# Pooled attention and two gated MLPs on one core: the second MLP's weight loads in pieces of 32 rows, low parts of the spatial inputs by VectorE, and another order of all steps

## The chip, the cores and the metric

The kernel runs on one core of a Trainium2 chip. The metric is the device time of one execution in microseconds (us). A core has five engines with their own instruction queues: TensorE (PE in the profile, with its weight loads as PEld), VectorE (DVE), ScalarE (ACT), GpSimd (POOL) and SyncE (SP), which here only starts DMA transfers. TensorE's clock has two levels, 1.2 and 2.4 GHz; the profile shows which share of full speed was granted (PEclk).

## The reference

Batch 8, sequence 576, width 512, 1024 inner columns. Three parts follow each other:

```python
# 1: attention over keys and values pooled by 8 (8 heads of 64)
attn = softmax(scale * q @ mean8(k).T);  x = attn @ mean8(v)
# 2: MLP with a gate from a convolution over the sequence
h = relu(x @ w_in)
g = h * sigmoid(conv3(h, conv_w));       x = g @ w_out
# 3: MLP with a spatial gate
h = gelu_tanh(x @ w_in2);  u, v = halves of h
v_n = (v - mean) / sqrt(var + 1e-6) * g_ln
v_s = einsum('ts,bsd->btd', w_sg, v_n) + b_sg
out = x + (u * v_s) @ w_out2
```

The weights come as 64-bit floats; the kernel reads them as pairs of 32-bit words and makes fp32 values of them with three integer instructions of VectorE (`to_f32`: one per line 146, 149 and 152).

## The kernel before, in words

Products run in fp32r, a format with fewer bits than fp32. To keep the precision each operand x is split into a high part h (a ScalarE cast) and a low part l = x - h (a subtraction, helper `subtract`, line 134, so every such subtraction stands at L134 in the profile), and a product takes three matmuls, hh, lh and hl. The tables `LO_X`, `LO_S`, `LO_G` and others (lines 109 to 114) name the engine that makes the low part of each operand: VectorE (`dve`) or GpSimd (`pool`).

Part 1 works batch by batch (steps k, v, q, s, e, a), and part 2 in 12 chunks of 384 columns. `t_i(f, c)` is the product of filter block f with chunk c, 12 matmuls into a bank of PSUM tag "i" (two banks, psi), and its epilogue: ScalarE's relu and centre tap, VectorE's two other taps (L569, L570), ScalarE's tanh, VectorE's g (L576, the last reader of the bank), then hg's high part on ScalarE and its low part on GpSimd. `t_o(f, c)` adds g @ w_out with 9 matmuls (L99 to L101) and writes the chunk to DRAM (`x2s`, L605).

When the attention is done, its SBUF tiles are released and the pool "w2" takes their place (`t_att_close`). Then `t_w2` loads the second MLP's input weight in eight pieces (w2raw, 512 KB each: half e of the columns, the rows of block kt) and converts each with three instructions of VectorE. Each half has three raw buffers for four loads, so the fourth load waits until the first is converted. `t_wsum` (GpSimd) and `t_wsplit` (ScalarE, VectorE) then make the seven combined weights of a Strassen-like scheme in which a 2 x 2 block product takes seven products (`products`). All this stands between chunks 9 to 11 of part 2.

Part 3 then reads x2s back transposed (`t_x2`), makes the seven combined inputs (`t_xc`), and computes u and v (`t_u`, `t_v2`), both stored to DRAM. The spatial stage goes by batch: `t_sc` makes seven combined spatial inputs sc of the normalised v, each a high and a low part; `t_sp` multiplies them with w_sg; its results gate u on GpSimd (L979); `t_g` splits the gated u into high and low parts (g for four full blocks of 128 rows, gr for the rest of 64 rows), and `t_o2` is the last product with the residual.

What sets the order: the string `ORDER` holds 3,617 steps. Each step is one call to `step`, which runs one generator up to its next `yield`, and every instruction that it issues is tied to the one before it on the same engine:

```python
            if ins.engine in last:
                tc.add_manual_dep(ins, last[ins.engine], pin, reason="order")
```

So each engine, and SyncE's queue of DMA issues, works strictly in the written order; a waiting instruction holds all that stand behind it on its engine. Semaphores between the engines follow from the data and from the buffers.

Of the kernel before, what the change touches and what calls it, by code (L numbers as in the profile page):

```python
# [26 lines left out]
def pooled_attention_gated_mlps(  # L27
# [23 lines left out]
    nc = tc.nc  # L51
    w_in, conv_w, w_out, w_in2, w_out2 = (a.bitcast(U32) for a in (w_in, conv_w, w_out, w_in2, w_out2))
    B, H, S, D = q.shape
# [6 lines left out]
    KC = DM // 128  # L60
# [5 lines left out]
    NM = S // 128  # L66
# [22 lines left out]
    def a_bank():  # L89
        return psum1.tile([128, 512], F32, tag="a", bufs=3, name="psa")  # L90
# [7 lines left out]
    def mm3(out_, ah, al, bh, bl, first, last):  # L98
        nc.tensor.matmul(out=out_, lhsT=ah, rhs=bh, start=first, stop=False)  # L99
        nc.tensor.matmul(out=out_, lhsT=al, rhs=bh, start=False, stop=False)  # L100
        nc.tensor.matmul(out=out_, lhsT=ah, rhs=bl, start=False, stop=last)  # L101

    def mm_sum(out_, pairs):
        n = len(pairs)
        for i, (a, b_) in enumerate(pairs):
            nc.tensor.matmul(out=out_, lhsT=a, rhs=b_, start=(i == 0), stop=(i == n - 1))  # L106

    dve, pool = nc.vector, nc.gpsimd
    LO_IN = [pool for f in range(NF)]
    LO_OUT = [pool for f in range(NF)]  # L110
    LO_E = [pool for b in range(B)]
    LO_X = {1: dve, 2: dve, 3: dve, 4: dve, 5: dve, 6: pool, 7: pool}
    LO_S = {1: dve, 2: dve, 3: pool, 4: dve, 5: dve, 6: dve, 7: pool}
    LO_G = [dve, dve, dve, pool, pool]
    ident = const.tile([128, 128], F32, name="ident")
    small = const.tile([128, 6], F32, name="small")
    mask, mhalf = small[0:96, 0:4], small[:, 4:6]
    coef = const.tile([128, 32], F32, name="coef")

    in1_ctx = ExitStack()  # L120
    in1 = in1_ctx.enter_context(tc.tile_pool(name="in1", bufs=1))
    att_ctx = ExitStack()
    att1 = att_ctx.enter_context(tc.tile_pool(name="att1", bufs=1, side="right"))
    att2 = att_ctx.enter_context(tc.tile_pool(name="att2", bufs=2, side="right"))
    KBT = att1.tile([128, NP_, 2 * SP], F32, name="KBT")
# [7 lines left out]
    def subtract(out, in0, hi, eng=nc.vector):  # L133
        eng.tensor_tensor(out=out, in0=in0, in1=hi.bitcast(F32), op=ALU.subtract)  # L134

    def to_f32(raw, t, tmp=None):

        w = raw.rearrange("p (n t) -> p t n", t=2)
        lo, up = w[:, 0, :], w[:, 1, :]
        ti = t.bitcast(U32)
        mi = ti if tmp is None else tmp.bitcast(U32)
        nc.vector.tensor_scalar(out=mi, in0=up, scalar1=3, scalar2=0x3FFFFFF8,
                                op0=ALU.logical_shift_left, op1=ALU.bitwise_and)
        yield
        nc.vector.scalar_tensor_tensor(out=mi, in0=up, scalar=0xC0000000, in1=mi,
                                       op0=ALU.bitwise_and, op1=ALU.bitwise_or)  # L150
        yield
        nc.vector.scalar_tensor_tensor(out=ti, in0=lo, scalar=29, in1=mi,
                                       op0=ALU.logical_shift_right, op1=ALU.bitwise_or)
        yield
# [454 lines left out]
    w2 = {}  # L609
# [5 lines left out]
    def split(dst, x, eng):  # L615
        nc.scalar.copy(out=dst[:, 0], in_=x)  # L616
        yield
        subtract(dst[:, 1], x, dst[:, 0], eng)
# [8 lines left out]
    def t_w2(i, *_):  # L627
        kt, e = i % KC, i // KC
        p = w2["p"]
        raw = p.tile([128, 1024], U32, tag=f"c{e}{4 + kt % 3}", name="w2raw")  # L630
        nc.sync.dma_start(
            out=raw, in_=w_in2[:, 1024 * e:1024 * e + 1024].rearrange("(c k i) n -> k c i n", k=KC, i=32)[kt])
        yield
        if kt % 2 == 0:
            wf[e, kt // 2] = p.tile([128, 2, 512], F32, tag=f"c{e}{kt // 2}", name="w2f")
        yield from to_f32(raw, wf[e, kt // 2][:, kt % 2, :], a_bank())
# [279 lines left out]
    def t_sc(m, b):  # L916
# [11 lines left out]
        sc[b, m] = w2["p"].tile([128, 2, 2, FH], F32R, tag=f"c0{m - 1}", name="sc")  # L928
        yield from split(sc[b, m], x, LO_S[m])

# [7 lines left out]
    g2 = {}  # L938
# [44 lines left out]
    def t_g(i, b):  # L983
# [12 lines left out]
        for h, l, y in hl:  # L996
            subtract(l, y, h, LO_G[i])

# [21 lines left out]
    def t_o2(i, b):  # L1020
# [14 lines left out]
        else:  # L1035
            for e in range(2):
# [4 lines left out]
    tasks = {"z": t_setup, "c": t_coef, "i": t_w_in, "t": t_w_out, "k": t_k, "K": t_kfin, "v": t_v, "V": t_vfin,  # L1041
             "q": t_q, "p": t_qtr, "s": t_s, "e": t_e, "x": t_x, "h": t_hg, "a": t_a, "I": t_i, "O": t_o, "A": t_att_close,
             "w": t_w2, "W": t_wsum, "Q": t_wsplit, "B": t_x2_open, "y": t_x2, "T": t_xc, "n": t_v2, "u": t_u,
             "g": t_sg, "G": t_sgsum, "H": t_sgsplit, "J": t_sgrest, "l": t_w_out2, "L": t_load, "S": t_sc, "R": t_vr,
             "b": t_bsg, "U": t_uload, "d": t_sp, "D": t_g, "m": t_res, "o": t_o2}
# [5 lines left out]
    def step(key):  # L1051

        if key not in running:
            i, _, b = key[1:].partition(".")
            running[key] = iter(tasks[key[0]](int(i or 0), int(b or 0)) or ())
        more = next(running[key], 0)
        issued = nc.cur_bb.bb.instructions
        for n in range(seen[0], len(issued)):
            ins = issued[n]
            if ins.engine in last:  # L1060
                tc.add_manual_dep(ins, last[ins.engine], pin, reason="order")
            last[ins.engine] = ins.name
        seen[0] = len(issued)
        return more is None

    for key in ORDER.split():
        step(key)
# [30 lines left out]
```

## Time and profile before

| | |
|---|---|
| median of 3 runs | 1012.65 us (1009.92 to 1012.85) |
| the profiled execution's own time | 1012.78 us |
| its span, first to last instruction | 1010.6 us |
| mean granted TensorE clock | 0.974 |
| busy TensorE / VectorE / GpSimd / ScalarE | 935.9 / 788.5 / 610.3 / 530.2 us |

The profile is of one execution. Names are out<-in with buffer numbers left out (w2raw is the weight piece of `t_w2`; in_moe_w_in_dram stands for both MLPs' input weights, since digits are dropped). A DMA share of 1 would be all 16 DMA engines busy. Where a busy TensorE runs at a granted clock below 1.00, its busy time is longer for the same work, so matmul counts are to be read beside it.

### The profile page before, as it was taken

The page shows a single profiled execution, that of the slowest core. Times are in us where ns is not written, and L with a number is a line of the kernel's source. Part 1 is how long each engine was busy: PE and PEld are TensorE (multiplying, and loading weights), DVE is VectorE, ACT ScalarE, POOL GpSimd, SP SyncE. Part 2 cuts the span into 40 slices and gives each one's busy share as a digit, 9 for nine tenths or more (in the row PEclk, how much of TensorE's full clock was granted, in tenths as well). Part 3 has the DMA queues.
Part 4 walks back from the last instruction along what each step waited for, and adds up shares of the span by engine and source line. Part 5 has one row for each costly group of instructions (what it writes and reads, how often), then busy time and mean ns, then how long its engine had stood idle before and what let it go on. Part 6 is the DMA issues. An engine that isn't in the chain of part 4 may idle for free.

```text
span 1010.6 us, 15826 instructions
## 1 busy us (share of the span) xinstructions
PE 935.9 (93%) x5396; PEld 853.9 (85%) x5396; DVE 788.5 (78%) x1351; ACT 530.2 (52%) x1108; POOL 610.3 (60%) x678
## 2 busy tenths in 40 slices
PE   5888899999999999999769979899899879999998
PEld 5786789899898998988658879889899869999996
DVE  5979987979888788886458469899776997767763
ACT  3755667676767667666236447556555332322211
POOL 3788687777777675473134256354542887776652
PEclk9899999999999999999779989999999999999999
DMA  9964263755637373231210574675366646565644
GB/s 241 269 195 95 79 151 102 169 149 132 171 108 163 87 153 108 66 103 59 104 59 32 100 118 119 160 199 129 112 171 220 205 138 184 179 206 172 202 141 135
DMA packets 182220, 143.60 MB, mean 142 GB/s; under 512 B 99296, under 2 KB 136444, under 8 KB 182140
## 3 DMA queue, kind: packets, MB, share of 16 engines
q1 hardware_dynamic: 182140, 142.61, 52.2%
q8 instruction: 42, 0.69, 0.3%
q14 instruction: 38, 0.31, 0.1%
HBM read 94.20 MB, written 48.37 MB: 141 GB/s over the span
## 4 chain that ended last, share of the span: by engine, by line
PE 62%; DVE 12%; POOL 7%; DMA 7%; SPq 4%; issue 3%; ACT 3%; POOLq 0%; DVEq 0%; ACTq 0%
PE psi L106 15%; PE pso L745 9%; PE psa L745 8%; PE pso L99 5%; PE pso L101 5%; PE pso L100 5%; DMA w2raw<-in_moe_w_in_dram 4%; PE psi L100 3%; PE psi L99 3%; PE psi L101 3%; PE psa L106 3%; PE psa L418 3%; POOL xb L692 1%; DVE vg L790 1%; DMA st<-in_v_dram 1%
## 5 line engine op out<-in xcount | busy, mean ns | idle before, releaser
L134 POOL TENSOR_TENSOR hg<-g,hg 128x384 fp32r<-128x384 f32 x96 | 101.7, 1064 | 91.2 <-ACT hg L579 91.0
L569 DVE SCALAR_TENSOR_TENSOR psi<-h,coef,psi 128x384 f32<-128x384 f32 x96 | 58.8, 612 | 36.7 <-ACT psi L567 35.9
L979 POOL TENSOR_TENSOR u<-u,tmp 128x288 f32<-128x288 f32 x64 | 61.6, 978 | 35.2 <-DVE tmp L975 24.8
L692 POOL TENSOR_TENSOR xb<-xb 128x768 f32<-128x768 f32 x24 | 47.8, 1996 | 56.5 <-DMA wsg<-in_moe_w_sg_dram 20.2
L572 ACT ACTIVATE psi<-psi 128x384 f32<-128x384 f32 x96 | 46.5, 484 | 63.4 <-DVE psi L570 63.2
L557 ACT ACTIVATE h<-psi 128x386 f32<-128x386 f32 (+1 forms) x96 | 47.3, 493 | 49.8 <-PE psi L106 49.6
L134 POOL TENSOR_TENSOR eTl<-xb,eTh 128x512 fp32r<-128x512 f32 (+1 forms) x30 | 44.9, 1496 | 44.1 <-ACT eTh L502 37.7
L570 DVE SCALAR_TENSOR_TENSOR psi<-h,coef,psi 128x384 f32<-128x384 f32 x96 | 59.8, 623 | 3.4
L576 DVE SCALAR_TENSOR_TENSOR g<-psi,h 128x384 f32<-128x384 f32 x96 | 52.4, 546 | 10.2 <-ACT psi L572 8.6
L579 ACT CAST hg<-g 128x384 fp32r<-128x384 f32 x96 | 47.9, 506 | 21.1 <-DVE g L576 20.7
L418 PE MATMUL psa<-KBT,qT 128*128 128x144 f32 (+1 forms) x320 | 54.8, 303 | 4.4 <-DVE eTl L134 2.1
L616 ACT CAST sc<-vf 128x512 fp32r<-128x512 f32 x48 | 29.0, 619 | 56.7 <-POOL vf L926 30.3
L745 PE MATMUL psa<-wc,xc 128*128 128x256 f32 x378 | 51.8, 284 | 7.0 <-DVE vg L773 6.7
L567 ACT ACTIVATE psi<-h,coef 128x384 f32<-128x384 f32 x96 | 56.3, 586 | 3.1
L745 PE MATMUL pso<-wc,xc 128*128 128x256 f32 x378 | 54.3, 293 | 3.3 <-ACT tmp L768 2.3
L745 PE MATMUL psa<-xc,wc 128*128 128x384 f32 x252 | 51.6, 348 | 5.4 <-ACT tmp L812 2.2
L418 PEld LDWEIGHTS psa<-KBT,qT 128*128 128x128 f32 (+1 forms) x320 | 46.3, 188 | 11.8 <-issue 2.9
L745 PEld LDWEIGHTS psa<-wc,xc 128*128 128x128 f32 x378 | 49.2, 189 | 8.1 <-DVE vg L773 7.3
L745 PEld LDWEIGHTS pso<-wc,xc 128*128 128x128 f32 x378 | 51.8, 198 | 4.2 <-ACT tmp L768 2.5
L745 PE MATMUL pso<-xc,wc 128*128 128x384 f32 x252 | 49.2, 338 | 2.8 <-DVE ub L822 2.2
L745 PEld LDWEIGHTS psa<-xc,wc 128*128 128x128 f32 x252 | 44.9, 197 | 6.9 <-ACT tmp L812 2.6
L697 ACT CAST xc<-xb 128x768 fp32r<-128x768 f32 x42 | 34.4, 836 | 27.8 <-POOL xb L692 13.8
(398 smaller groups left out, 3182.4 us busy)
## 6 DMA issues: line engine op xcount, KB each, us to landing
xb<-eds SPq DMA_DIRECT2D x24, 384.0 KB
x2s<-ob SPq DMA_DIRECT2D x36, 256.0 KB
xb<-x2s SPq DMA_DIRECT2D x48, 192.0 KB
us<-ub SPq DMA_DIRECT2D x24, 384.0 KB
vs<-vg SPq DMA_DIRECT2D x18, 512.0 KB
u<-us SPq DMA_DIRECT2D x16, 576.0 KB
vf<-vs SPq DMA_DIRECT2D x16, 512.0 KB
out_dram<-ob SPq DMA_DIRECT2D x32, 256.0 KB
```

Of the source, the lines that this page charges most:

```text
L99: nc.tensor.matmul(out=out_, lhsT=ah, rhs=bh, start=first, stop=False)
L100: nc.tensor.matmul(out=out_, lhsT=al, rhs=bh, start=False, stop=False)
L101: nc.tensor.matmul(out=out_, lhsT=ah, rhs=bl, start=False, stop=last)
L106: nc.tensor.matmul(out=out_, lhsT=a, rhs=b_, start=(i == 0), stop=(i == n - 1))
L134: eng.tensor_tensor(out=out, in0=in0, in1=hi.bitcast(F32), op=ALU.subtract)
L418: nc.tensor.matmul(out=ps[0:n, 2 * SP * x:2 * SP * x + 2 * SP], lhsT=qT[:, p, 0:n], rhs=KBT[:, p, :], start=True, stop=True)
L567: nc.scalar.activation(out=y, in_=tap(1), func=AF.Copy, scale=cw(1, f))
L569: nc.vector.scalar_tensor_tensor(out=y, in0=tap(0), scalar=cw(0, f), in1=y, op0=ALU.mult, op1=ALU.add)
L570: nc.vector.scalar_tensor_tensor(out=y, in0=tap(2), scalar=cw(2, f), in1=y, op0=ALU.mult, op1=ALU.add)
L692: pool.tensor_tensor(out=x, in0=y, in1=z, op=ALU.subtract)
L745: nc.tensor.matmul(out=ps, lhsT=a, rhs=b_, start=first and i == 0, stop=last and i == n - 1, skip_group_check=True)
L979: pool.tensor_tensor(out=z, in0=z, in1=o, op=ALU.mult)
```

## The change

`t_w2` issues four DMAs per load, each of 32 rows into 32 partitions, instead of one whose source is a pattern of 4 blocks by 32 rows. The low parts of all spatial inputs sc and of all gated blocks g and gr are made by VectorE; before, GpSimd made sc of products 3 and 7, the fourth g and gr. And `ORDER` is another sequence of the same 3,617 steps.

```diff
-ORDER = '''z k0.0 k1.0 k2.0 z z p0.0 c p1.0 p2.0 v0.0 v1.0 p3.0 p4.0 v2.0 i0 i1 z z k0.1 k1.0 k2.0
...
+ORDER = '''z k0.0 k1.0 k2.0 z z p0.0 c p1.0 p2.0 v0.0 v1.0 p3.0 p4.0 v2.0 i0 i1 z z k0.1 k1.0 p0.1
...
-    LO_S = {1: dve, 2: dve, 3: pool, 4: dve, 5: dve, 6: dve, 7: pool}
-    LO_G = [dve, dve, dve, pool, pool]
+    LO_S = {m: dve for m in range(1, 8)}
+    LO_G = [dve for i in range(NM + 1)]
...
-        nc.sync.dma_start(
-            out=raw, in_=w_in2[:, 1024 * e:1024 * e + 1024].rearrange("(c k i) n -> k c i n", k=KC, i=32)[kt])
+        for c in range(4):
+            r0 = 128 * c + 32 * kt
+            nc.sync.dma_start(out=raw[32 * c:32 * c + 32], in_=w_in2[r0:r0 + 32, 1024 * e:1024 * e + 1024])
```

SyncE's queue at the end of the attention, before (-) and after (+), eds and xb being attention's scores on their way through DRAM and x2s the chunks of part 2:

```order
+L605 DMA x2s_82<-ob 128x512
 L466 DMA eds_118<-en 64x4x128
 L467 DMA eds_118<-en 64x4x64
 L496 DMA xb<-eds_118 128x384
 L605 DMA x2s_83<-ob 128x512 x2
-L631 DMA w2raw<-in_moe_w_in_dram 128x1x1024 x8
+L633 DMA w2raw<-in_moe_w_in_dram 32x1024 x32
 L605 DMA x2s_83<-ob 128x512
 L605 DMA x2s_84<-ob 128x512 x3
 L605 DMA x2s_85<-ob 128x512 x3
```

The eight loads become 32 issues at the same place; the third store of the same chunk stands behind them in both.

VectorE at the first two conversions of w2raw, before (numbers tell buffers apart: w2raw_5385 is the first load, w2raw_5404 the second, w2raw_5416 the third; psi and g belong to the epilogues of part 2):

```order
L576 SCALAR_TENSOR_TENSOR g_5419<-psi_5388,h_5401 128x384
L146 TENSOR_SCALAR psa_5425<-w2raw_5385 128x512
L149 SCALAR_TENSOR_TENSOR psa_5425<-w2raw_5385,psa_5425 128x512
L146 TENSOR_SCALAR psa_5457<-w2raw_5404 128x512
L152 SCALAR_TENSOR_TENSOR w2f_5424<-w2raw_5385,psa_5425 128x512
L569 SCALAR_TENSOR_TENSOR psi_5440<-h_5453,coef_121,psi_5440 128x384
L570 SCALAR_TENSOR_TENSOR psi_5440<-h_5453,coef_121,psi_5440 128x384
L149 SCALAR_TENSOR_TENSOR psa_5457<-w2raw_5404,psa_5457 128x512
L146 TENSOR_SCALAR psa_5464<-w2raw_5416 128x512
L152 SCALAR_TENSOR_TENSOR w2f_5456<-w2raw_5404,psa_5457 128x512
L576 SCALAR_TENSOR_TENSOR g_5482<-psi_5440,h_5453 128x384
```

The same place after (w2raw_5424 is the first load, w2raw_5433 the second; xl is the low part of an attention output):

```order
L576 SCALAR_TENSOR_TENSOR g_5422<-psi_5335,h_5367 128x384
L146 TENSOR_SCALAR psa_5430<-w2raw_5424 128x512
L149 SCALAR_TENSOR_TENSOR psa_5430<-w2raw_5424,psa_5430 128x512
L152 SCALAR_TENSOR_TENSOR w2f_5429<-w2raw_5424,psa_5430 128x512
L532 SCALAR_TENSOR_TENSOR xl_489<-psa_5358,xh_372 128x288
L146 TENSOR_SCALAR psa_5458<-w2raw_5433 128x512
L576 SCALAR_TENSOR_TENSOR g_5471<-psi_5389,h_5402 128x384
L569 SCALAR_TENSOR_TENSOR psi_5440<-h_5453,coef_121,psi_5440 128x384
L570 SCALAR_TENSOR_TENSOR psi_5440<-h_5453,coef_121,psi_5440 128x384
L149 SCALAR_TENSOR_TENSOR psa_5458<-w2raw_5433,psa_5458 128x512
L576 SCALAR_TENSOR_TENSOR g_5497<-psi_5440,h_5453 128x384
L152 SCALAR_TENSOR_TENSOR w2f_5457<-w2raw_5433,psa_5458 128x512
```

Before, the first instruction of the second load stands ahead of the next epilogue, and that of the third ahead of that epilogue's g; after, the first load is converted in one go, and a whole epilogue stands between the first and the last instruction of the second load.

GpSimd at the end of the first combined inputs of batch 1 and the first gated blocks of batch 0, before (vf and sf are spatial inputs, u the gated product):

```order
L926 TENSOR_TENSOR vf<-sf,vf 128x2x256
L979 TENSOR_TENSOR u_8283<-u_8283,tmp_8591 128x288
L979 TENSOR_TENSOR u_8315<-u_8315,tmp_8568 128x288
L926 TENSOR_TENSOR vf<-vf 128x2x256
L134 TENSOR_TENSOR sc<-vf,sc 128x512 x2
L134 TENSOR_TENSOR g<-u_8315,g 128x2x128
L134 TENSOR_TENSOR g<-u_8283,g 128x2x128
L134 TENSOR_TENSOR gr<-u_8315,gr 128x2x64
L134 TENSOR_TENSOR gr<-u_8283,gr 128x2x64
L979 TENSOR_TENSOR u_8542<-u_8542,tmp_8728 128x288
```

The same place after:

```order
L927 TENSOR_TENSOR vf<-sf,vf 128x2x256
L980 TENSOR_TENSOR u_8475<-u_8475,tmp_8546 128x288
L980 TENSOR_TENSOR u_8305<-u_8305,tmp_8611 128x288
L980 TENSOR_TENSOR u_8475<-u_8475,tmp_8572 128x288
L927 TENSOR_TENSOR vf<-vf 128x2x256
L927 TENSOR_TENSOR sf<-vf 128x512
L980 TENSOR_TENSOR u_8751<-u_8751,tmp_8717 128x288
```

The four kinds of L134 rows are gone from GpSimd; they stand among VectorE's instructions now, and the sums for the next batch follow at once.

## Rows read from the trace of the kernel before

**Rows 1.** the page, head and section 1

```profile
span 1010.6 us, 15826 instructions
PE 935.9 (93%) x5396; PEld 853.9 (85%) x5396; DVE 788.5 (78%) x1351; ACT 530.2 (52%) x1108; POOL 610.3 (60%) x678
```

**Rows 2.** stretches: us; PE, PEld, DVE, ACT, POOL busy (count); PEclk, DMA share, GB/s

```profile
25.00:150.00 125.00, 108.32 (x648) 93.74 (x647) 111.71 (x207) 76.33 (x175) 96.74 (x126) 0.93 0.63 156
150.00:475.00 325.00, 324.65 (x1756) 294.63 (x1755) 267.08 (x493) 221.21 (x441) 223.95 (x276) 1.00 0.47 122
475.00:530.00 55.00, 38.45 (x160) 34.35 (x159) 29.31 (x51) 18.28 (x38) 11.87 (x12) 0.81 0.21 81
530.00:565.00 35.00, 34.71 (x173) 31.05 (x172) 26.67 (x38) 22.21 (x45) 16.31 (x13) 1.00 0.06 23
785.00:835.00 50.00, 41.77 (x275) 39.01 (x276) 48.84 (x78) 17.62 (x39) 40.61 (x37) 0.97 0.56 173
835.00:1000.00 165.00, 165.00 (x970) 149.51 (x969) 113.91 (x189) 45.62 (x111) 108.32 (x110) 1.00 0.59 182
```

**Rows 3.** chain of waits, 470 to 600 us; start us, us, what

```profile
475.42 17.47 DMA w2raw<-in_moe_w_in_dram
495.39 22.92 DMA w2raw<-in_moe_w_in_dram
```

**Rows 4.** waits, 470 to 530 us; us in total, times, longest us

```profile
DVE psa L146 <- DMA w2raw<-in_moe_w_in_dram: 22.1, 6, 6.7
PE psi L106 <- DVE g L576: 16.5, 4, 6.9
```

**Rows 5.** timeline of VectorE; start us, us, what, [idle before <- releaser]

```profile
482.81 0.70 DVE L146 TENSOR_SCALAR psa<-w2raw 128x512 uint32<-128x512 uint32 x1 [2.88 <-DMA w2raw<-in_moe_w_in_dram]
498.00 0.69 DVE L146 TENSOR_SCALAR psa<-w2raw 128x512 uint32<-128x512 uint32 x1 [0.97 <-DMA w2raw<-in_moe_w_in_dram]
```

**Rows 6.** timeline of SyncE's queue, 465 to 540 us

```profile
474.13 25.66 SPq L631 DMA_DIRECT2D w2raw<-in_moe_w_in_dram  x8
499.83 37.51 SPq L605 DMA_DIRECT2D x2s<-ob  x4
```

**Rows 7.** busy time by stretch; and SyncE's v loads, ns min/median/max

```profile
495.00:500.00 5.00, 5.00 (x16) 5.00 (x17) 3.86 (x7) 1.65 (x4) 1.01 (x1) 0.50 0.25 102
676.00:678.00 2.00, 2.00 (x19) 1.99 (x18) 2.00 (x5) 1.16 (x4) 0.00 (x0) 1.00 1.04 405
233.00:238.00 5.00, 5.00 (x25) 4.34 (x24) 4.86 (x11) 3.42 (x7) 2.92 (x4) 1.00 0.64 198
L233 SPq DMA_DIRECT2D raw<-in_v_dram x48: 311/425/1801, 66.2 to 355.7; - x48
```

**Rows 8.** line L134, whole span; duration ns min/median/max, first and last start us

```profile
L134 DVE TENSOR_TENSOR g<-u,g x48: 409/694/1516, 819.4 to 996.0; 128x256 fp32r<-128x256 f32 x48
L134 DVE TENSOR_TENSOR sc<-vf,sc x32: 657/808/1774, 772.8 to 979.8; 128x512 fp32r<-128x512 f32 x32
L134 POOL TENSOR_TENSOR sc<-vf,sc x16: 1280/1402/1804, 790.7 to 967.0; 128x512 fp32r<-128x512 f32 x16
L134 POOL TENSOR_TENSOR g<-u,g x16: 732/742/1189, 819.1 to 993.6; 128x256 fp32r<-128x256 f32 x16
L134 POOL TENSOR_TENSOR gr<-u,gr x16: 454/462/907, 820.9 to 994.7; 128x128 fp32r<-128x128 f32 x16
```

**Rows 9.** by line and shape, 785 to 835 us; busy us, mean ns, idle before

```profile
L134 DVE TENSOR_TENSOR sc<-vf,sc 128x512 fp32r<-128x512 f32 x8 | 10.1, 1262 | 0.0
L134 DVE TENSOR_TENSOR g<-u,g 128x256 fp32r<-128x256 f32 x7 | 6.8, 1005 | 0.0
L134 POOL TENSOR_TENSOR sc<-vf,sc 128x512 fp32r<-128x512 f32 x4 | 6.2, 1574 | 0.0
```

**Rows 10.** chain of waits, 792 to 832 us

```profile
812.27 1.70 POOL sc L134
```

**Rows 11.** busy time by stretch, 715 to 720 us

```profile
715.00:720.00 5.00, 2.28 (x15) 1.87 (x13) 4.57 (x4) 1.63 (x3) 4.74 (x4) 1.00 0.00 0
```

2 lines of the change are left out of this document (1 added, 1 removed).

## The prediction, made before the changed kernel was run

> **What bounds the kernel now.** I read the page's first two sections, then the busy time of each engine by stretch, then the chain of waits and the list of waits in the one long stretch where TensorE is not full, and last the two stretches at 785 us and after it. TensorE is busy for 93% of the span [rows 1]. By stretch [rows 2]: from 150 to 475 us it is full (324.65 of 325 us), and so it is from 835 to 1000 us (165 of 165); from 475 to 530 us it works only 38.45 of 55 us, at a mean granted clock of 0.81, while the DMA share is 0.21 and every other engine has idle time too; from 785 to 835 us it works 41.77 of 50 us while VectorE is at 48.84 and GpSimd at 40.61 of 50. The reader is to see that the hole at 475 us has no full engine, so something is being waited for, and that the one at 785 us has a full VectorE.
>
> In the hole the chain of waits is nearly all one transfer, w2raw, in pieces of 17.47 and 22.92 us [rows 3]; VectorE waits 22.1 us for it, and TensorE 16.5 us for VectorE's g [rows 4]. VectorE runs in a written order, and the first of three conversion instructions for each of the eight w2raw loads stands ahead of the epilogues of the convolution MLP that free TensorE's PSUM banks: a late load stops the epilogue, and that stops TensorE. VectorE gets the loads at 482.81, ..., 498.00 us, four of them 5.06 us apart [rows 5], 512 KB each: 104 GB/s. In those stretches the DMA share is 0.25, four of 16 engines [rows 7].
>
> **The change, part by part.** *The loads in pieces.* Before, the source of a w2raw load is a pattern of 4 blocks by 32 rows by 4 KB; after, each of four DMAs takes one block, 32 rows of 4 KB, to 32 partitions. Two loads of before are near that shape. A piece of the second MLP's output weight, also 512 KB in rows of 4 KB, but with 128 rows as the outer dimension, goes beside a store of u at a share of 1.04 and 405 GB/s; the v loads, in pieces of 32 rows, go at 198 GB/s and a share of 0.64 over 5 us that are not full of them [rows 7]. These are my bounds for the pieces, 198 to 405 GB/s: 4 MB in 10 to 21 us instead of 8 x 5.06 = 40.5. The Trainium skill's page "DMA: Bandwidth & Descriptors" (section "Why a DMA increments its semaphore by 16 and not by 1") says that the number of DMA engines is the largest up to 16 that divides the slowest dimension of both sides. By that rule it is 4 before, which the trace's 0.25 bears out, and 16 after, which no row of before shows for this source; the time would be the forecast's. SyncE pays: 32 issues of 0.425 us, the median of the v pieces [rows 7], 13.6 us. So a whole load goes out every 1.7 us and arrives every 1.7 to 2.6. The first load of before took 482.81 - 474.13 - 5.06 = 3.6 us beyond its transfer [rows 5, 6]; with the same, the eight are there by 474.1 + 21 + 3.6 = 499 us at the latest, where before they took until about 474.1 + 40.5 + 3.6 = 518. Between the conversions of two loads stands about one epilogue, for which TensorE has 12 + 9 matmuls, 21 x 0.2006 = 4.2 us (the price is worked out below); so at TensorE's pace the order asks for a load every 4 us, and I count no wait for w2raw any more. What stands behind the issues on SyncE is a store of x2s; before it left at 499.83 us [rows 6], so 474.1 + 13.6 = 487.7 costs nothing. If a conversion of the first loads were late, the loads that reuse their buffer would hold that store.
>
> What the hole is worth: 160 matmuls in 55 us; the next stretch, same work, same two loops, does 173 in 34.71 busy us at clock 1.00 [rows 2]: 0.2006 us each, 32.1 us for 160. So 55 - 32.1 = 22.9 us are lost: 16.55 in which TensorE stands still, 6.35 because it then works at the lower of its two clock levels (granted clock 0.50, 1.2 of 2.4 GHz, from 495 to 500 us, 16 matmuls where 5 / 0.2006 = 25 fit [rows 7]; the longest standstill before such a start is 6.9 us [rows 4]). Not all comes back: VectorE has 29.31 us of work there, 91% of 32.1. In the stretch from 150 to 475 us VectorE is at 82% and TensorE loses nothing; from 25 to 150 us it is at 89% and TensorE loses 16.7 of 125 us, 13% [rows 2]. Bounds of what stays: 0 and 13% of 32.1 = 4.3 us. I take 3, by the nearer row. Term: **-19.9 us**. The weight splits that follow on VectorE and GpSimd come earlier with the loads, and first serve the products of part 3.
>
> *Low parts from GpSimd to VectorE.* Per batch two sc subtractions (m = 3 and 7), two g and two gr: 48 instructions. GpSimd gives up 16 x 1.402 + 16 x 0.742 + 16 x 0.462 = 41.7 us by its medians [rows 8]. VectorE takes the same shapes at 0.657 (sc) and 0.409 (g) at the least, 0.808 and 0.694 at the median [rows 8], 1.262 and 1.005 where GpSimd is busy beside it [rows 9]; gr is half of g, my estimate 0.2, 0.35 and 0.5. In all 20.3, 29.6 or 44.3 us. From 835 us on TensorE is full, VectorE has 113.91 of 165; its share of the new work, some 13/16 of 29.6 = 24 us, makes 84%, as in the stretch where TensorE lost nothing. I cost that at nothing; the cover is TensorE's own work.
>
> From 785 to 835 us there is no such cover. Four sc, two g and two gr of GpSimd stand there (g and gr are of batch 0) [rows 9]. With VectorE as the bound this costs 4 x 0.657 + 2 x 0.409 + 2 x 0.2 = 3.8 us at the least and 8.1 at contended prices. With GpSimd as the bound (its sc is on the chain at 812.27 us [rows 10]) it gives back: if each moved instruction only changes a GpSimd time for a lone VectorE time, 4 x (1.574 - 0.657) + 2 x (0.742 - 0.409) + 2 x (0.462 - 0.2) = 4.9 us [rows 8, 9]. VectorE's sc at 1.262 us where 0.657 is possible shows that the two engines slow each other. The Trainium skill's page "SBUF — State Buffer" (section "Who interferes with whom") says that a VectorE instruction with two SBUF inputs and a GpSimd instruction that reads SBUF exclude each other for the whole instruction. By that rule the shorter instruction frees the pair, and the sum below would be 988.0; by VectorE's busy row alone it would be 996.7 to 1001. Without it the bounds are -4.9 and +8.1; VectorE is the fuller engine, but its durations hold the waits that GpSimd's work causes, so I take **0**, between them.
>
> *The order.* 3,617 steps before and after, the same steps. The large places stay (the first conversion of w2raw, the first transposition of x2 and the first sc stand 9 to 14 rows earlier among some 1,300 of VectorE); what moves is local. It can open or close holes like the one at 715 to 720 us, 2.72 us [rows 11]; two of these either way, so I take 0 and keep +-5.
>
> Sum, against the profiled execution's own time: 1012.8 (span 1010.6 [rows 1] and 2.2 around it) - 19.9 = **992.9 us**; the runs' median is 0.1 lower. I predict 993.
>
> **Rivals.**
> (1) Only half comes back. VectorE at 91% with conversions in front of epilogues still makes TensorE wait, and the loads that reuse a buffer still wait for a conversion. For it: VectorE's share, and 25 to 150 us. Against: in 150 to 475 us TensorE kept full beside a VectorE at 82%. 1012.8 - 11.5 = 1001.3.
> (2) The pieces don't spread, or go as slowly as before because each reaches only 32 partitions: 1012.8, and by local order 1009 to 1016. For it: the v pieces at half of the best rate. Against: 198 GB/s is still nearly twice 104. The Trainium skill's page "SBUF — State Buffer" (section "The DMA setup-cost knee") speaks for this rival: transfers should use 128 partitions and be as large as they can. No row here shows a load of 128 KB to 32 partitions by itself.
> (3) More than forecast: nothing stays of the 22.9 and GpSimd's relief counts fully, 1012.8 - 22.9 - 4.9 = 985.0.
> (4) Slower: VectorE becomes the bound from 785 us on. At contended prices 44.3 us come on top of its 48.84 + 113.91 in 215 us. If the last stretch then behaves like 25 to 150 us (VectorE 89%, TensorE loses 13%), that is 22 us of 165, with the 8.1 before it: 1012.8 - 19.9 + 30.1 = 1023. It decides from a VectorE share of about 89% on; against it, fewer GpSimd instructions mean fewer contended prices, and 84% is what the medians give.
>
> **How the numbers follow.** Forecast 0.66 (own range 987 to 999: the order's +-5 and what stays), (1) 0.15, (2) 0.06, (3) 0.08, (4) 0.05. The range of 8 in 10 reaches from 984, just beyond (3), to 1004, beyond (1). This kernel can be told from no change at about 0.3%, 3 us. Faster: the forecast, (1), (3) and a third of (2), 0.91; the same 0.04; slower (4) and a little of (2), 0.05.
>
> **What would show it.** Right: VectorE's waits for w2raw under 3 us in all; the stretch with the eight conversions done in 32 to 36 us at clock 1.00; a DMA share well over 0.25 there; the opening of x2 some 20 us earlier; TensorE still full in the last 150 us. Wrong: w2raw still on the chain; TensorE waiting for g there for more than 5 us; or VectorE over 90% and TensorE with holes behind 835 us (in before's clock).

## The result, and the profile after

The changed kernel takes 980.9 us (median of 4 runs, 979.3 to 982.9); the kernel before took 1012.75 us beside it (4 runs, 1009.9 to 1014.3). The ratio is 0.969, 95% interval 0.9662 to 0.9718. It is faster, as forecast, but by 31.8 us and not by 19.9: the time lies below the low end of the range, 984.

The head of the page and its first section, after:

```profile
span 978.8 us, 15842 instructions
PE 925.9 (95%) x5396; PEld 843.8 (86%) x5396; DVE 785.7 (80%) x1399; ACT 530.4 (54%) x1108; POOL 564.1 (58%) x630
```

Against [rows 1], TensorE's busy time fell by only 10.0 us and the span by 31.8: most of the gain is standstill that went. VectorE has 48 instructions more and 2.8 us less busy time; GpSimd lost 46.2 us.

Busy time by stretch, after (columns as in [rows 2]). The first two stretches are the same times as there, 475 to 480 us lies in the loads, and the others are chosen at about the same places of the program:

```profile
25.00:150.00 125.00, 110.86 (x667) 95.48 (x667) 114.09 (x211) 79.91 (x181) 96.23 (x128) 0.96 0.67 163
150.00:475.00 325.00, 323.23 (x1748) 293.04 (x1748) 261.86 (x492) 218.92 (x438) 224.41 (x276) 1.00 0.47 123
470.00:505.00 35.00, 34.09 (x173) 30.97 (x172) 30.46 (x53) 18.79 (x40) 13.50 (x13) 1.00 0.50 128
475.00:480.00 5.00, 5.00 (x26) 4.60 (x27) 4.74 (x9) 2.19 (x5) 1.10 (x2) 1.00 1.02 240
752.00:802.00 50.00, 44.26 (x294) 41.22 (x293) 45.17 (x83) 18.71 (x41) 29.97 (x28) 0.97 0.61 191
802.00:967.00 165.00, 164.29 (x970) 148.86 (x969) 129.46 (x230) 47.05 (x114) 78.12 (x73) 1.00 0.57 182
```

The hole of before is gone: from 470 to 505 us TensorE does 173 matmuls in 34.09 busy us at clock 1.00, what the undisturbed stretch of [rows 2] did in 34.71. While pieces arrive the DMA share is 1.02 and 240 GB/s, against 0.25 and 102 in [rows 7]. The last stretch does the same 970 matmuls as in [rows 2], though VectorE went from 113.91 to 129.46 us in it.

The first instructions on w2raw, by form (count, duration ns min/median/max, first and last start), and all that waited for it (us, times); then SyncE's queue; then TensorE's wait for VectorE's g from 465 to 525 us:

```profile
L633 SPq DMA_DIRECT2D w2raw<-in_moe_w_in_dram x32: 310/419/496, 469.8 to 486.5; - x32
L146 DVE TENSOR_SCALAR psa<-w2raw x8: 682/687/689, 474.7 to 499.3; 128x512 uint32<-128x512 uint32 x8
who waited for it (us, times):
  POOL ws L647: 2.9, 1
```

```profile
469.81 17.10 SPq L633 DMA_DIRECT2D w2raw<-in_moe_w_in_dram  x32
487.02 55.33 SPq L605 DMA_DIRECT2D x2s<-ob  x7
```

```profile
PE psi L106 <- DVE g L576: 0.9, 1, 0.9
```

VectorE does not wait for w2raw once (22.1 us in [rows 4]), TensorE waits 0.9 us for g instead of 16.5, and SyncE has issued all loads in 17.1 us instead of 25.66 [rows 6]; the 32 issues were priced at 13.6, and the difference cost nothing here, since the store behind them left at 487.02 us.

To see where the 31.8 us lie, I took the first start of some instructions from the views by tile and subtracted them along the program (us; the last row is the span):

| stretch of the program | before | pieces alone | after | after less before |
|---|---|---|---|---|
| start to first load of w2raw | 474.1 | 474.7 | 469.8 | -4.3 |
| to first load of xb (x2 opens) | 96.9 | 74.4 | 73.8 | -23.1 |
| to first product on x2 | 12.5 | 12.5 | 10.1 | -2.4 |
| to first product on sc | 204.6 | 204.1 | 204.8 | +0.2 |
| to the end | 222.5 | 222.9 | 220.3 | -2.2 |
| span | 1010.6 | 988.6 | 978.8 | -31.8 |

The second row is the forecast's hole. Nearly all of its 22.9 us came back: 23.1 us in the changed kernel's trace and 22.5 in the trace with the pieces alone. The rest, 8.7 us, stands in rows for which the forecast had only "0 +-5".

### The profile page after: what moved, and what is told of

Same layout as the page of the kernel before. It is cut to its first block, busy times and chain, and to the rows that moved or that the text cites. A ratio compares the mean times of both kernels' runs of the same rounds, so it can differ in the third digit from the quotient of the medians.

```text
span 978.8 us, 15842 instructions
## 1 busy us (share of the span) xinstructions
PE 925.9 (95%) x5396; PEld 843.8 (86%) x5396; DVE 785.7 (80%) x1399; ACT 530.4 (54%) x1108; POOL 564.1 (58%) x630
## 4 chain that ended last, share of the span: by engine, by line
PE 68%; DVE 14%; DMA 8%; SPq 4%; issue 3%; ACT 2%; POOL 2%; DVEq 0%; ACTq 0%; POOLq 0%
PE psi L106 18%; PE psa L746 9%; PE pso L746 8%; PE pso L99 6%; PE pso L101 6%; PE pso L100 6%; PE psi L100 3%; PE psi L99 3%; PE psi L101 3%; DMA xb<-x2s 3%; PE psa L418 3%; PE psa L106 3%; DMA st<-in_v_dram 1%; DMA qb<-in_q_dram 1%; DVE sc L134 1%
## 5 line engine op out<-in xcount | busy, mean ns | idle before, releaser
L134 POOL TENSOR_TENSOR hg<-g,hg 128x384 fp32r<-128x384 f32 x96 | 100.9, 1057 | 77.9 <-ACT hg L579 77.2
L693 POOL TENSOR_TENSOR xb<-xb 128x768 f32<-128x768 f32 x24 | 45.7, 1905 | 47.5 <-DVE xc L134 21.4
L134 POOL TENSOR_TENSOR eTl<-xb,eTh 128x512 fp32r<-128x512 f32 (+1 forms) x30 | 46.4, 1545 | 43.9 <-ACT eTh L502 41.4
L579 ACT CAST hg<-g 128x384 fp32r<-128x384 f32 x96 | 47.7, 506 | 15.2 <-DVE g L576 13.7
L746 PE MATMUL pso<-wc,xc 128*128 128x256 f32 x378 | 52.0, 285 | 3.8 <-POOL xc L134 2.1
L746 PEld LDWEIGHTS pso<-wc,xc 128*128 128x128 f32 x378 | 49.0, 190 | 5.2 <-ACT tmp L769 2.5
L995 ACT CAST g<-u 128x256 fp32r<-128x256 f32 x64 | 22.1, 403 | 45.8 <-POOL u L980 35.2
```

Of the source, the lines that this page charges most:

```text
L746: nc.tensor.matmul(out=ps, lhsT=a, rhs=b_, start=first and i == 0, stop=last and i == n - 1, skip_group_check=True)
```

## The experiments

Ratios are to the kernel before, timed beside it on the same chip; since that kernel's own median is not the same each time (1011.1 to 1013.2 us), "us" in the table below is ratio times 1012.7. The eight cases are every combination of the three parts, with the 95% interval of the ratio in brackets.

| loads | low parts | old order | new order |
|---|---|---|---|
| one DMA | GpSimd | 1012.7 | 0.9857 (0.9838 to 0.9876): 998.2 |
| one DMA | VectorE | 1.0150 (1.0134 to 1.0165): 1027.9 | 0.9828 (0.9810 to 0.9845): 995.3 |
| pieces | GpSimd | 0.9796 (0.9779 to 0.9813): 992.0 | 0.9689 (0.9670 to 0.9707): 981.2 |
| pieces | VectorE | 0.9934 (0.9919 to 0.9949): 1006.0 | after: 0.9690 (0.9662 to 0.9718): 981.3 |

**The pieces alone (e1), the order alone (e2), both (e3).** e1 takes the first of these hunks, e2 the string (only its first steps are shown), e3 both:

```diff
-        nc.sync.dma_start(
-            out=raw, in_=w_in2[:, 1024 * e:1024 * e + 1024].rearrange("(c k i) n -> k c i n", k=KC, i=32)[kt])
+        for c in range(4):
+            r0 = 128 * c + 32 * kt
+            nc.sync.dma_start(out=raw[32 * c:32 * c + 32], in_=w_in2[r0:r0 + 32, 1024 * e:1024 * e + 1024])
...
-ORDER = '''z k0.0 k1.0 k2.0 z z p0.0 c p1.0 p2.0 v0.0 v1.0 p3.0 p4.0 v2.0 i0 i1 z z k0.1 k1.0 k2.0
+ORDER = '''z k0.0 k1.0 k2.0 z z p0.0 c p1.0 p2.0 v0.0 v1.0 p3.0 p4.0 v2.0 i0 i1 z z k0.1 k1.0 p0.1
```

> The kernel before with one thing of the change: the w2raw loads in four pieces of 32 rows. Theory A (the hole at 475 us is the transfer alone, and the old order is as good as the new one once the loads are quick): 1012.7 - 20 to 23 = 990 to 993 us, VectorE's waits for w2raw under 3 us where they were 22.1. Theory B (the loads help only together with the new order of VectorE's conversions and epilogues): about half comes back, 1000 us or more, TensorE waits for g over 8 us between the first conversion and the last. Theory C (the pieces themselves don't matter): 1010 to 1015.

> The kernel before with the new order alone: loads of w2raw in one DMA with 4 blocks as outer dimension, low parts on GpSimd as before. Theory A: the order is worth what lies outside the hole, the 4.3 us by which the first w2raw load left earlier and some 4 behind the opening of x2: 1003 to 1007 us, with the hole as before (VectorE waits 20 us or more for w2raw). Theory B (the new order alone takes the waiting out by asking later for the loads): 995 or less. Theory C (the order outside the hole is worth nothing by itself): 1010 to 1015.

> The changed kernel with the low parts of sc, g and gr on GpSimd as before: pieces and new order. Theory A (the moved low parts are worth nothing): 979 to 983 us, as the changed kernel. Theory B (the moved low parts give back 2 to 5 us in the stretch where the spatial stage begins): 983 to 987. Theory C (they cost, VectorE being the fuller engine there): 974 to 978.

Measured: 991.07, 998.43 and 981.46 us. The pieces' share is as forecast (theory A of e1). The order is not: it is worth 14.5 us alone, between theories A and B of e2, and 10.8 beside the pieces (theory A of e3). Part of what it gives alone is the hole itself; VectorE's wait for the loads, with the old loads in the new order (us, times, longest):

```profile
DVE psa L146 <- DMA w2raw<-in_moe_w_in_dram: 12.2, 3, 8.8
```

It was 22.1 us in [rows 4] with the same DMAs: the new order asks for a load later, and so takes up some of what the pieces would give. In the traces with pieces nothing of that wait is left to take, so the 10.8 us come from elsewhere.

**Order and low parts without the pieces (e4).**

```diff
-    LO_S = {1: dve, 2: dve, 3: pool, 4: dve, 5: dve, 6: dve, 7: pool}
-    LO_G = [dve, dve, dve, pool, pool]
+    LO_S = {m: dve for m in range(1, 8)}
+    LO_G = [dve for i in range(NM + 1)]
...
-ORDER = '''z k0.0 k1.0 k2.0 z z p0.0 c p1.0 p2.0 v0.0 v1.0 p3.0 p4.0 v2.0 i0 i1 z z k0.1 k1.0 k2.0
+ORDER = '''z k0.0 k1.0 k2.0 z z p0.0 c p1.0 p2.0 v0.0 v1.0 p3.0 p4.0 v2.0 i0 i1 z z k0.1 k1.0 p0.1
```

> The changed kernel with the old w2raw loads: new order and low parts on VectorE. Theory A (pieces, order and low parts add up): 980.9 + 20 to 23 = 1001 to 1004 us, with VectorE waiting 18 us or more for w2raw and the DMA share at 0.25 there. Theory B (the new order asks later for the loads, so the pieces matter less in it): 990 to 997.

Measured: 994.78 us (theory B). In the changed kernel, undoing the pieces costs 14.0 us, undoing the low parts (e3) nothing.

**Which steps of the order (e5 to e8).** Four orders made of a head of one string and, behind the cut, what is left of the other; all with pieces, low parts on GpSimd. The cut of e5 is the first step of w2raw (w4 and w0 behind it), that of e8 the first step y0.0, which opens x2. Of each string only the place of the cut is shown, - the old one, + the run's:

```diff
-a2.7 I6.9 I6.9 a3.7 A I5.9 w4 a2.7
+a3.7 a2.6 I4.9 O0.9 I6.9 I6.9 O7.7 O6.7 O5.8 w4 w0 a3.7 w2 I7.9
...
-O4.11 I7.11 B I5.11 I7.11 I6.11 y0.0 y0.0 O3.10 y0.0
+O4.11 I7.11 B I5.11 I7.11 I6.11 O0.10 W0.1 O1.10 O6.10 O7.10 O6.9 y0.0 y0.0
```

> Loads in pieces, low parts on GpSimd as before; the new order for every step up to the first load of w2raw, and from there the old order of the steps that are left. It lies between pieces with the old order (991.07 us) and pieces with the new order (981.46 us). Theory A (the order's 9.6 us are made before the loads: in the stretch from 125 to 150 us TensorE is busy for 24.77 us with the new order and 21.97 with the old one): 981 to 984 us. Theory B (spread, in the shares in which the landmarks of the two traces part: 3.3 of 6.8 us before the loads, 2.8 up to the first product on x2, 0.7 behind it): 985.5 to 988 us. Theory C (made behind the loads): 989.5 to 992 us.

> The other way round: pieces, low parts on GpSimd, the old order up to the first load of w2raw and the new order of the steps that are left. Theory A (the gain lies before the loads): 989 to 992 us. Theory B (spread): 984.5 to 987.5 us. Theory C (behind the loads): 981 to 983 us. If this run and the one with the new order in front don't add up to 9.6 us below 991.07, the two halves are not independent.

> Pieces, low parts on GpSimd, the new order up to the first step that opens x2 (its loads into xb), the old order behind it. Theory A and theory B both: 981 to 984 us, since at most 0.7 us of the traces' difference lie behind the first product on x2. Theory C in its form that the second MLP gains: 987 us or more.

> Pieces, low parts on GpSimd, the old order up to the first step that opens x2, the new order behind it. Theory A and B: 988.5 to 991.5 us. Theory C in its form that the second MLP gains: 985 us or less.

Measured: 985.47, 987.07, 986.27 and 984.43 us; by ratios, 6.2, 5.3, 5.8 and 7.4 us less than the pieces alone, each +-3 by the intervals. The two halves of each cut add up to the whole within that, so the gain is spread (theory B of e5 and e6, e5 at its edge). Of e7 and e8 theory C came nearer than A and B: the steps behind the opening of x2 are worth about as much as those ahead. The landmarks say where: from the first load of w2raw to the first product on x2 it takes 86.9 and 87.3 us in e5 and e7 (old order at the opening), 83.3 in e6 and e8 (new order), 86.9 in e1 and 84.1 in e3. Up to that load traces of one order differ by up to 5 us (old 473.1 to 478.0 in eight traces, new 468.8 to 473.0 in eight), the means by 4.4.

**Two single steps (e9, e10).** Both are e1 with one thing moved in the old string:

```diff
-I0.1 t6 t6 V.2 V.2 s0.2 O2.0
+I0.1 t6 t6 V.2 s0.2 O2.0
...
-s3.2 s2.2 t7 e0.2 V.2 I2.1
+s3.2 s2.2 t7 V.2 e0.2 V.2 I2.1
...
-y1.0 y1.0 g4 O1.10 g1 y1.0 T1.0 W0.1 O7.11 T1.0 T3.0
+y1.0 T1.0 T1.0 y1.0 g4 O1.10 g1 y1.0 W0.1 O7.11 T3.0
```

> Pieces with the old order and low parts on GpSimd (991.07 us), and one step moved: GpSimd's four subtractions of Vl (4.38 us together in that trace) stand behind the low parts of the output weights w6 and w7, and not ahead of them. Theory A (the order's gain ahead of the loads is this one wait: TensorE waits 2.89 us for w6hl with the old order and not at all with the new one): 987 to 989 us, and the first load of w2raw is issued 2 to 3 us earlier than at 474.7. Rival B (the next late thing takes its place, eTl or Vl itself): 990 to 992.5 us.

> Pieces with the old order and low parts on GpSimd (991.07 us), and one step moved: the cast and the low part of the first xc stand ahead of the transpositions of the second batch of x2 on ScalarE and VectorE, and not behind them. In the old order VectorE waits for that batch's transfer until 559.4 us and makes the first low part at 561.2; the first product comes 12.5 us after the first load of xb, with the new order 9.0 to 10.3 us. Theory A (this stall in VectorE's order is what the new order saves at the opening of x2): 987 to 988.5 us, first product 9 us or less after the first load. Rival B (the first product comes earlier, but the next ones wait for GpSimd's subtractions as before): first product earlier, time 990 to 992 us.

Measured: 989.82 and 989.84 us, ratios 0.9768 (0.9755 to 0.9782) and 0.9778 (0.9763 to 0.9792): 1 to 3 us each. Theory A falls in both. e9 comes out as its rival B says, though 0.2 us below that range: TensorE's wait for w6hl went from 2.9 to 1.0 us, but its waits for g in the same stretch came to 2.1, that for eTl stayed at 1.8, and the first load of w2raw is issued at 475.1 us, no earlier than the 474.7 of e1. TensorE's waits from 95 to 150 us in e9:

```profile
PE psi L106 <- DVE g L576: 2.1, 3, 1.0
PE psa L106 <- DVE eTl L134: 1.8, 1, 1.8
...
PE pso L101 <- POOL w6hl L134: 1.0, 1, 1.0
```

In e10 the first product comes no earlier, so rival B falls too. VectorE makes the first low part at 559.1 us, but the first product starts at 562.51, 12.5 us after the first load of xb as in e1. TensorE's timeline, first in e10 and then in the changed kernel:

```profile
562.29 0.39 PE L101 MATMUL pso<-w7hl,hg 128*128 128x512 f32 x1
562.51 1.22 PE L746 MATMUL psa<-xc,wc 128*128 128x384 f32 x6
565.25 0.61 PE L746 MATMUL psa<-xc,wc 128*128 128x384 f32 x2 [1.51 <-ACT xc L698]
```

```profile
553.66 0.62 PE L746 MATMUL psa<-xc,wc 128*128 128x384 f32 x2 [0.43 <-ACT xc L698]
556.70 1.65 PE L746 MATMUL psa<-xc,wc 128*128 128x384 f32 x4 [2.42 <-DVE xc L134]
558.14 0.63 PE L99 MATMUL pso<-w6hl,hg 128*128 128x512 f32 x1
...
562.76 0.39 PE L101 MATMUL pso<-w7hl,hg 128*128 128x512 f32 x1
562.99 1.23 PE L746 MATMUL psa<-xc,wc 128*128 128x384 f32 x6
```

In the old order TensorE itself is late: its last products of part 2 (L99 to L101) all stand ahead of the first product on x2, so when the inputs of the second one are not ready there is nothing left to do. The new order puts the first product among them, and 18 of part 2's matmuls still fill the time up to 562.99. I had read the wait at VectorE; by the timelines it was TensorE's own order. No run moves that one product alone, so this is read and not shown.

**The low parts alone (e12), with pieces (e13), and with the new order behind x2 alone (e15).** All have this hunk; e13 and e15 the pieces too, and e15 e8's string:

```diff
-    LO_S = {1: dve, 2: dve, 3: pool, 4: dve, 5: dve, 6: dve, 7: pool}
-    LO_G = [dve, dve, dve, pool, pool]
+    LO_S = {m: dve for m in range(1, 8)}
+    LO_G = [dve for i in range(NM + 1)]
```

> The kernel before with nothing but the low parts of sc, g and gr on VectorE. Theory A (covered by TensorE's work; what VectorE pays at 785 us GpSimd gives back): 1010.5 to 1014 us. Rival B (GpSimd is the bound at 785 us): 1008 to 1010 us. Rival C (VectorE becomes the bound): 1016 us and more.

> Pieces and low parts on VectorE, the old order. Theory A (the low parts' cost comes from where they stand in VectorE's order behind 785 us, and has nothing to do with the loads): 991.1 + 15.3 = 1006 us, 1003 to 1009. Rival B (with the loads no longer late, VectorE has the time): 990 to 994 us.

> Pieces, low parts on VectorE, the old order up to the first step that opens x2 and the new order behind it. With the low parts on GpSimd the same order took 984.4 us. Theory A (the steps behind the opening of x2 alone take the low parts' cost away): 983 to 986.5 us. Rival B (the steps ahead of it are needed too): 990 us or more.

Measured: 1028.2, 1003.78 and 983.27 us. In the old order the low parts cost 15.2 us without and 14.0 with the pieces (theory A of e13); with the steps behind the opening of x2 in the new order they cost nothing (theory A of e15: 985.0 by its ratio, e8 984.6). Rival C of e12 has the time right but not the cause. VectorE did not become the bound: it is busy for 58.94 + 43.59 of the 145 us from 840 to 985, 71%, less than the 78% of the changed kernel's last stretch. Yet TensorE loses time there:

```profile
840.00:925.00 85.00, 79.45 (x457) 71.56 (x456) 58.94 (x111) 21.46 (x51) 37.52 (x34) 0.96 0.54 169
925.00:985.00 60.00, 57.94 (x338) 51.98 (x337) 43.59 (x81) 19.25 (x47) 27.23 (x26) 1.00 0.57 180
```

One such loss, followed back in e12's timelines. VectorE, ScalarE and SyncE (start us, us, what, [idle before <- releaser]):

```profile
848.50 0.75 DVE L134 TENSOR_TENSOR g<-u,g 128x256 fp32r<-128x256 f32 x2
853.37 0.49 DVE L134 TENSOR_TENSOR gr<-u,gr 128x128 fp32r<-128x128 f32 x2 [4.13 <-ACT gr L994]
853.78 0.51 DVE L975 SCALAR_TENSOR_TENSOR tmp<-psa,coef,tmp 128x288 f32<-128x288 f32 x1
```

```profile
852.52 0.62 ACT L616 CAST sc<-vf 128x512 fp32r<-128x512 f32 x1 [6.54 <-DMA vf<-vs]
853.05 0.49 ACT L994 CAST gr<-u 128x128 fp32r<-128x128 f32 x2
```

```profile
841.11 5.54 SPq L1034 DMA_DIRECT2D out_dram<-ob  x2
847.54 0.38 SPq L909 DMA_DIRECT2D vf<-vs  x1
```

A load of vf stands behind two stores of the output on SyncE and leaves at 847.54 us; ScalarE's cast of sc waits 6.54 us for it, and the cast of gr behind it is late; VectorE waits 4.13 us for that cast, and the evictions (tmp) behind it wait too. TensorE's longest wait for a tmp, 4.8 us, is this one (it goes on at 854.78 us). Its waits for the tmp of that bank behind 780 us:

```profile
PE pso L745 <- DVE tmp L975: 6.9, 5, 4.8
```

In the kernel before, gr's low part was GpSimd's, so its wait for the cast (4.9 us in all) stood in GpSimd's queue and not ahead of VectorE's evictions. By line and shape, VectorE's low parts behind 775 us (busy us, mean ns | idle before), first e12, then the changed kernel:

```profile
L134 DVE TENSOR_TENSOR sc<-vf,sc 128x512 fp32r<-128x512 f32 x48 | 39.0, 821 | 9.1 <-ACT sc L616 8.9
L134 DVE TENSOR_TENSOR g<-u,g 128x256 fp32r<-128x256 f32 x64 | 33.1, 561 | 4.0 <-ACT g L994 4.0
L134 DVE TENSOR_TENSOR gr<-u,gr 128x128 fp32r<-128x128 f32 x16 | 5.7, 396 | 6.2 <-ACT gr L994 6.2
```

```profile
L134 DVE TENSOR_TENSOR sc<-vf,sc 128x512 fp32r<-128x512 f32 x40 | 35.6, 906 | 0.0
L134 DVE TENSOR_TENSOR g<-u,g 128x256 fp32r<-128x256 f32 x64 | 33.3, 566 | 0.0
L134 DVE TENSOR_TENSOR gr<-u,gr 128x128 fp32r<-128x128 f32 x16 | 6.8, 469 | 0.0
```

The durations are no shorter in the changed kernel. What differs is the wait ahead of them: 19.3 us against none (0.2 with the eight sc that start before 775 us there; 0.2 in e15 as well, where only the steps behind the opening of x2 are new). TensorE's waits for tmp go with it: 9.5 us in e12 and 14.6 in e13, where the low parts cost 15.2 and 14.0, against 3.6 in the kernel before, 3.1 in e15 and 2.8 in the changed kernel. All of TensorE's waits behind 780 us are 18.1 us in e12 and 8.4 in the kernel before; the other third of the loss is not followed back here, and the granted clock fell to 0.96 from 840 to 925 us.

**Loads in two DMAs of two blocks (e14).** The changed kernel with

```diff
-        for c in range(4):
-            r0 = 128 * c + 32 * kt
-            nc.sync.dma_start(out=raw[32 * c:32 * c + 32], in_=w_in2[r0:r0 + 32, 1024 * e:1024 * e + 1024])
+        for c in range(2):
+            src = w_in2[256 * c:256 * c + 256, 1024 * e:1024 * e + 1024].rearrange("(c k i) n -> k c i n", k=KC, i=32)
+            nc.sync.dma_start(out=raw[64 * c:64 * c + 64], in_=src[kt])
```

> The changed kernel (980.9 us), but each load of w2raw as two DMAs of 64 partitions, each of 2 blocks by 32 rows; 256 KB per DMA. Theory A (the outer dimension of a DMA sets how many of the 16 engines it uses: 2 here, 4 in the kernel before, 16 or more for a piece of 32 rows): share 0.125 for one DMA alone, 0.25 at most for two side by side; the loads come no faster than one per 5 us, as before, and VectorE waits for them: 993 to 1003 us. Rival B (smaller DMAs are faster because more of them run side by side): share clearly over 0.25, time 980 to 985 us.

Measured: 1036.71 us, ratio 1.0248 (1.0223 to 1.0273). It is slower than even theory A said:

```profile
475.00:480.00 5.00, 4.39 (x21) 3.73 (x21) 0.56 (x2) 1.99 (x4) 0.34 (x1) 1.00 0.13 52
...
490.00:495.00 5.00, 0.00 (x0) 0.00 (x0) 0.46 (x1) 0.00 (x0) 0.00 (x0) 0.50 0.13 52
```

```profile
470.58 8.72 SPq L633 DMA_DIRECT2D w2raw<-in_moe_w_in_dram  x5
```

The share is 0.13, two of 16 engines, and 52 GB/s. At that rate the 8.72 us of SyncE's first five issues (256 KB each) bring in less than two of them, so several were outstanding, and the others add nothing. Twice the DMAs, half the rate. So it is not the number of DMAs that made the loads fast but the shape of each: 2, 4 and 32 in the outer dimension give 0.13, 0.25 and 1.02. Size (256, 512 and 128 KB) and partitions (64, 128 and 32) do not order the three so. The rule of the Trainium skill that the prediction drew on, in "DMA: Bandwidth & Descriptors" (section "Why a DMA increments its semaphore by 16 and not by 1"), says also that the lowest-numbered engines are taken; DMAs that don't add up agree with that.

**VectorE at the opening of x2 (e11).** The experiments point to GpSimd there: in the changed kernel its chain of four subtractions and two low parts runs from 557.66 to 570.9 us, at about 2 us each, while VectorE takes 0.91 to 1.05 for each of its first two low parts (1.67 to 1.89 for the later ones, beside GpSimd) and has gaps. The changed kernel with e10's move and

```diff
-            pool.tensor_tensor(out=x, in0=y, in1=z, op=ALU.subtract)
+            (dve if k == 0 else pool).tensor_tensor(out=x, in0=y, in1=z, op=ALU.subtract)
...
-        subtract(l, x, h, LO_X[m])
+        subtract(l, x, h, dve if k == 0 else LO_X[m])
```

> The changed kernel (980.9 us) with three edits at the opening of x2, batch 0 only: the cast and low part of the first xc ahead of the transpositions of the second batch, the four subtractions on xb on VectorE and not on GpSimd, and the two low parts of xc that GpSimd makes on VectorE too. Theory A (from 557.7 to 570.8 us GpSimd's chain of four subtractions of 1.85 us and two low parts of 2.15 us is what TensorE waits for, while VectorE has long gaps and takes 0.92 us for one): 975 to 978.5 us. Rival B (the transfer into xb and the casts decide): 980 to 982 us. Rival C (VectorE's written order makes its own instructions late): over 982 us.

Measured: 978.26 us (977.2 to 979.3), ratio 0.9659 (0.9646 to 0.9673): in theory A's range, and the fastest of all. From 540 to 600 us, e11 first, then the changed kernel:

```profile
540.00:600.00 60.00, 55.16 (x319) 49.34 (x318) 46.59 (x68) 32.95 (x64) 21.40 (x19) 1.00 0.65 135
```

```profile
540.00:600.00 60.00, 53.06 (x295) 48.41 (x294) 38.38 (x55) 31.17 (x60) 31.99 (x23) 0.94 0.64 131
```

TensorE does 24 matmuls more in the same time, and its clock no longer falls there. The two ratios' intervals overlap a little (0.9662 to 0.9673), so by the times alone the gain, 3.1 us by the ratios and 2.6 by the medians, is likely, not shown.

## Why the prediction was wrong

- **What bounds the kernel**: right. The hole was the loads, and nearly all of it came back with them.
- **The pieces, -19.9**: right in mechanism; the pieces alone give 20.7 us (18.9 to 22.4). The 3 us put down as "what stays" are not in the traces, where 0.4 stays (22.9 less 22.5); the times alone would allow them. With VectorE at 30.46 of 35 us (87%) TensorE was busy for 34.09 in the changed kernel. So the 13% lost from 25 to 150 us was no measure for this stretch; VectorE's share alone does not set the loss. The step "at TensorE's pace the order asks for a load every 4 us" held, and the pieces came within the bounds, 240 GB/s.
- **The low parts, 0**: right in the changed kernel, wrong as worked out. The reason given was that TensorE's own work covers VectorE's up to a share of 84 to 89%. In the old order they cost 14 to 15 us at 71%. What decides is whether VectorE must wait ahead of them, and that is the order's doing (e13 against e15).
- **The order, 0 +-5**: this is the step that failed. It was priced as "two of these either way", as if a new order could only shuffle small holes. It gives 10.8 us beside the pieces and, since it is what makes the low parts free, 24.7 us beside pieces and low parts together (1006.0 to 981.3). The reading was of places ("the large places stay", 9 to 14 rows earlier), not of who waits at them. [rows 2] had shown the size of what there was to take: 16.7 us from 25 to 150 us and 8.2 from 785 to 835. In the same stretches 14.1 and 5.7 us are still lost after the change. By the landmarks the order's gain is some 4.4 us ahead of the loads (mean of eight traces each), 2.4 to 3.6 from the loads to the first product on x2, and some 2 from the first product on sc to the end.
- **The rivals**: (3), "more", 985.0, came nearest, but for a wrong reason: GpSimd's relief gave nothing (e3 and the changed kernel are equal). (2) fell by e1: loads of 128 KB to 32 partitions went at 227 GB/s there (480 to 485 us, share 1.06), where 512 KB to 128 had gone at 104. (1) fell by the full hole. (4) saw that the low parts can cost, at twice the size (22 + 8.1 us against the 14 to 15 measured in the old order) and with the wrong cause, a full VectorE. What kept it away is the order, not the share.
- **The signs**: waits for w2raw under 3 us, 32 to 36 us at clock 1.00, a share far over 0.25 and a full TensorE at the end are all there; the opening of x2 came 27.4 us earlier, where 20 was the sign for the forecast, so the landmark told the difference at once.

Left open: which moves make the 4.4 us ahead of the loads and the 2 at the end. One single step ahead of the loads did not (e9), and the place of the first load varies by up to 5 us between traces of one order. From 100 to 175 us TensorE does 366 and 368 matmuls in the old order (before, e1) and 383 and 391 in the new (e3, changed kernel), so much of the 4.4 lies there.

## What to carry to other kernels

Where each engine works in a written order, an edit that moves work between engines is not priced by busy shares: ask what the moved instruction waits for at its place in the new queue, and who stands behind it. So price the edit in the order that it will run in, and try every combination of the parts before adding their effects up. For a load, look at the DMA share: 0.25 with nothing else under way was a matter of shape here, and cutting the load smaller along the wrong dimension made it worse.

## What the runs showed of the hardware that was not expected

- Several DMAs of SyncE's queue, outstanding together and each with an outer dimension of 2, stayed at a share of 0.13 and 52 GB/s in all (e14); those of 32 rows went at 1.02 and 240 GB/s. A full share is not yet the best rate: in the kernel before the same share moved 405 GB/s [rows 7]. Why is open; the loads are not alike in shape, and a store ran beside the faster one.
- VectorE's subtractions got shorter when GpSimd no longer made its own: the median for g went from 0.694 [rows 8] to 0.418 us, for sc from 0.808 to 0.684, in the old order too (e12). So 48 more instructions cost VectorE's total nothing in the changed kernel (788.5 to 785.7 us). The Trainium skill's page "SBUF — State Buffer" (section "Who interferes with whom") says that the two engines lock a shared port pair; the shorter durations agree, and here it was worth busy time, not time.
